# Attention output turned by VectorE and ScalarE instead of TensorE, from the fourth group on, in a fused DeltaNet and gated-MLP kernel

## The chip, the cores and the metric

The kernel runs on one core of a Trainium2 chip. The metric is the time of one execution on the device in microseconds (us); lower is better. In the profile PE is TensorE's matmul, PEld its weight load, DVE is VectorE, ACT is ScalarE, POOL is GpSimd and SP is SyncE.

## The reference, cut to what matters

```python
# q, k, v: (4, 8, 768, 48) = batch, heads, tokens, head size; all f32
k_n = k / (norm(k) + 1e-6)
for t in range(768):
    y[t]  = q[t] @ state                                   # per batch and head, state is 48 x 48
    state = state + beta[t] * outer(k_n[t], v[t] - k_n[t] @ state)
x   = y as (batch * token, 8 * 48)                         # 3072 x 384
out = (sigmoid(x @ w_gate) * (x @ w_val)) @ w_out          # 384 -> 1536 -> 384
```

## The kernel before

The 768 tokens are cut into 12 groups (0 to 11) of 64 tokens for each of the 4 batches, so a group has 256 tokens. Two kinds of work are woven into one instruction order that is written out by hand.

**The MLP of one group** is 12 tiles of the hidden width. For each, `gate_val` multiplies x of the group by 128 columns of both first weights (18 products of 128x256, into a two-buffered PSUM tile `gv`). ScalarE takes the sigmoid of one half (`sg`), VectorE multiplies it by the other half, ScalarE and VectorE split the product into two fp32r parts (`h`), and two tiles later `outp` multiplies them by the second weight (6 products of 128x384, into `po`). Every operand is split into a high and a low fp32r part, so x is a tile `xx` with a high half `xh` and a low half `xl`; the first product of a group reads `xh` and the second reads `xl`.

**The attention of the next group** runs in the gaps: key products (`gram`), norms and a triangular solve on VectorE (`solve`, many small operations on `X`, `gp` and `tmp`), the state's part (`rest`, `updates`, `advance`) and the output rows (`rows`). `rows` writes Y into PSUM (`yy`) with tokens on the partitions, and ScalarE copies it to `ys`, 128 x 768. The MLP needs Y with features on the partitions, in `xx`.

**The order.** A slot is one half of an MLP tile: an even slot issues `gate_val`, an odd slot issues `outp`. Lists say what else is issued in a slot: `plan[s]` right behind the matmuls, `late[s]` at its end. A group's MLP takes 24 slots; for group g, `w = 24 (g-1)` is the slot in which the MLP of the group before it starts, so its own starts at `w + 24`. For groups 3 to 11, `rows` and `advance` of the group stand in slot `w + 16`, and the turning of Y (`flip`) in `w + 18`. `scaling` puts 16 ScalarE operations on `kv` of a later group (`kv` times a norm, four per slot) into four slots. `spread` deals the small solve operations over slots by the room that the table `busy` leaves. No scheduler moves anything: every engine runs its queue in this order, and an instruction that waits holds up all behind it on its engine.

**Turning Y before the change.** `flip` runs twice, for 128 tokens each: three TensorE transpositions of 128x128 into PSUM (`pt`), then ScalarE rounds `pt` to `xh` and VectorE writes the rest to `xl`.

Of the kernel before, what the change touches and what calls it, by code (L numbers as in the profile page):

```python
# [12 lines left out]
F32 = mybir.dt.float32  # L13
F32R = mybir.dt.float32r
# [5 lines left out]
ALU = mybir.AluOpType  # L20
AX = mybir.AxisListType
PSUM = bass.MemoryType.PSUM

B, H, S, D = 4, 8, 768, 48
C = 64
GT = B * C
# [18 lines left out]

DM = H * D
FF = 1536
KC = DM // 128
# [7 lines left out]
def deltanet_gated_mlp(ctx: ExitStack, tc: tile.TileContext, kd, qd, kv, beta, words, out):  # L56
    nc = tc.nc
# [4 lines left out]
    wk = ctx.enter_context(tc.tile_pool(name="wk", bufs=1))  # L62
# [21 lines left out]
    state = [{} for _ in range(N)]  # L84
# [8 lines left out]
    def beat(ins):  # L93
        beats.append(ins)

    def busy_array(out, n, after=()):

        for i in range(n):
            ins = nc.tensor.matmul(out=out.rearrange("q a b -> q (a b)"), lhsT=flat[:, 0:128], rhs=flat, start=True, stop=True)  # L99
            if i < len(after):  # L100
                pace(ins, after[i])
# [20 lines left out]
    def load_group(g):  # L122
        load_k(g)
        load_q(g)
        load_rows(g, 1)
        load_rows(g, 0)
# [246 lines left out]
    def solve_halves(g):  # L373


        st = state[g]
        gp, gam = st["gp"], st["gam"]
        X = st["X"]
        H = wk.tile([128, 2, 8, 16], F32, name=f"H_{g}", tag="H", bufs=1)
        gs = wk.tile([128, 2, 16, 16], F32, name=f"gs_{g}", tag="gs", bufs=1)  # L380
        for b in range(2):
            nc.vector.tensor_tensor(out=H[:, b], in0=dmask[:, 8 * b:8 * b + 8, 16 * b:16 * b + 16],
                                    in1=gam[:, 16 * b:16 * b + 16].unsqueeze(1).to_broadcast([128, 8, 16]), op=ALU.mult)
            yield
            nc.vector.scalar_tensor_tensor(out=gs[:, b], in0=gp[:, 16 * b:16 * b + 16, 16 * b:16 * b + 16], scalar=-1.0,
                                           in1=gam[:, 16 * b:16 * b + 16].unsqueeze(1).to_broadcast([128, 16, 16]), op0=ALU.mult, op1=ALU.mult)
            yield
        for j in range(15, 0, -1):
            k, n = j // 2, 8 - j // 2
            tmp = wk.tile([128, 2, n, j], F32, name=f"tmp_{g}_{j}", tag="tmp", bufs=2)  # L390
            beat(nc.vector.tensor_tensor(out=tmp, in0=H[:, :, k:8, j:j + 1].to_broadcast([128, 2, n, j]),
                                         in1=gs[:, :, j:j + 1, 0:j].to_broadcast([128, 2, n, j]), op=ALU.mult))
            yield
            beat(nc.vector.tensor_tensor(out=H[:, :, k:8, 0:j], in0=H[:, :, k:8, 0:j], in1=tmp, op=ALU.add))
            yield
        for b in range(2):
            nc.vector.tensor_copy(out=X[:, 8 * b:8 * b + 8, 16 * b:16 * b + 16], in_=H[:, b])
            yield
        A, D, Z = (joints[g][:, i] for i in range(3))
        nc.vector.transpose(mt.rearrange("q c (k r) -> q k c r", r=2), X.rearrange("q k (c r) -> q k c r", r=2))  # L400
        yield
        pool, tag = (ps_aux, "aux") if g else (ps_gv, "gv")
        pz, pm = (pool.tile([128, CP, 32], F32, name=f"{n}_{g}", tag=tag) for n in ("pz", "pm"))

        def blocks(out, lhsT, rhs):
            for c in range(CP):
                for r in range(0, 128, 32):
                    nc.tensor.matmul(out=out[r:r + 32, c], lhsT=lhsT[r:r + 32, c], rhs=rhs[r:r + 32, c], start=True, stop=True)  # L408
        if g == 0:
            paced = beats[8::2]  # L410
            busy_array(pz, len(paced) + 4, after=paced)
        if g:
            blocks(pz, A, mt)
        else:
            for c in range(CP):
                for r in range(0, 128, 64):
                    nc.tensor.matmul(out=pz[r:r + 64, c], lhsT=wide[r:r + 64, c], rhs=mt[r:r + 64, c], start=True, stop=True)
        if g == 0:
            busy_array(pm, 2)
        yield  # L420
        nc.vector.transpose(D.rearrange("q c t -> q (c t)"), mt.rearrange("q c t -> q (c t)"))
        nc.scalar.copy(Z, pz)
        yield
        blocks(pm, D, Z)
        if g == 0:
            gap.append(ps_gv.tile([128, J, C], F32, name="gap", tag="gv"))
            busy_array(gap[0], 3)
        yield
        st["joint"] = nc.vector.tensor_tensor(out=mt, in0=mt, in1=pm, op=ALU.subtract)
        yield  # L430
# [101 lines left out]
    def flip(g, c):  # L532

        st = state[g]
        if c == 0:
            xx = wk.tile([128, 2, KC, GT], F32R if g else F32, name=f"xx_{g}", tag=f"xx{(g + 1) % 2}", bufs=1)
            st["xh"], st["xl"] = (xx[:, i] for i in range(2))
        xh, xl, ys = st["xh"], st["xl"], st["ys"][:, c].rearrange("p h e d -> p (h e d)")
        pt = ps_aux.tile([128, KC, 128], F32, name=f"pt_{g}_{c}", tag="aux")
        for k in range(KC):  # L540
            nc.tensor.transpose(pt[:, k], ys[:, k * 128:(k + 1) * 128], ident)  # L541
        ts = slice(c * 128, (c + 1) * 128)
        if g == 0:
            (nc.vector.tensor_copy if c else nc.scalar.copy)(out=xh[:, :, ts], in_=pt)  # L544
            return
        nc.scalar.copy(xh[:, :, ts], pt)
        nc.vector.tensor_tensor(out=xl[:, :, ts], in0=pt, in1=xh[:, :, ts].bitcast(F32), op=ALU.subtract)


    def gate_val(g, f):  # L550
        st = state[g]
        x = (st["xh"], st["xl"])
        st["gv", f] = pg = ps_gv.tile([128, 2, GT], F32, name=f"gv_{g}_{f}", tag="gv")
        for o, w in ((0, "g"), (1, "v")):
            for k in range(KC):
                if g == 0:
                    nc.tensor.matmul(out=pg[:, o], lhsT=parts[w, f][:, k * 128:(k + 1) * 128], rhs=x[0][:, k], start=k == 0, stop=k == KC - 1)  # L557
                    continue
                for q, (a, b) in enumerate(((0, 0), (0, 1), (1, 0))):
                    nc.tensor.matmul(out=pg[:, o], lhsT=parts[w, f][:, a, k * 128:(k + 1) * 128], rhs=x[b][:, k], start=(k == 0 and q == 0), stop=(k == KC - 1 and q == 2))  # L560
# [43 lines left out]
    plan = collections.defaultdict(list)  # L604
    late = collections.defaultdict(list)

    def steps(gen, n=1):
        def fn():
            for _ in range(n):
                next(gen, None)  # L610
        return fn
# [10 lines left out]
    def chain(*gens):  # L622
        for q in gens:
            yield from q
# [5 lines left out]
    def scaling(g, s):  # L630
        for i in range(4):
            plan[s + i].append(steps(scalings[g], 4))
# [88 lines left out]
    busy = collections.Counter()  # L721

    def mask_later(g, s):
        def fn():
            masks = masked(g)
            take(masks, 2)
            plan[s + 1].insert(0, steps(masks, 2))
        late[s].append(fn)
        for i in range(2):
            busy[s + i] += 1.4  # L730
# [9 lines left out]
    for g in range(N):  # L740
        w = W * (g - 1)
        if g == 0:
            late[3].append(lambda: advance(0))
            continue
        up, at_rows = (13, 19) if g < 3 else (10, 16)
        at_rest = {1: 8, 2: 28}.get(g, w + 6)
        late[at_rest].append(lambda g=g: rest(g))
        for step in range(3):
            late[w + up + 2 * step].append(lambda g=g, step=step: updates(g, step))
        late[w + at_rows].append(lambda g=g: rows(g))  # L750
        late[w + at_rows].append(lambda g=g: advance(g))
        for c in range(2):
            late[w + at_rows + 2].append(lambda g=g, c=c: flip(g, c))
            busy[w + at_rows + 2] += 0.6
        busy[at_rest] += 1.1
        busy[w + up + 2] += 1.1
        busy[w + at_rows] += 1.1
        busy[w + at_rows + 1] += 1.1
        if g == 1:
            mask_later(1, 11)  # L760
        else:
            if g > 2:
                plan[w - 27].append(lambda g=g: load_group(g))
            gram_later(g, {2: 3, 3: 32}.get(g, w - 18))
            mask_later(g, w + 1 if g == 2 else w - 12)
            if g > 2:
                solves.append((g, w - 13 if g == 3 else w - 14, w + 9))
            scaling(g, {2: 25, 3: 43}.get(g, w - 7))
    spread(chain(norms(2), halves2), NORMS + 36, 8, 25, lambda s: max(0.1, 1.6 - busy[s]))
    for at in (26, 29, 30, 30, 31):  # L770
        plan[at].append(steps(halves2))
# [74 lines left out]
```

## Time and profile before

| what | value |
|---|---|
| median of 3 runs | 649.55 us (645.4 to 651.54) |
| the profiled execution: time, span of its instructions | 646.87 us, 645.2 us |
| mean granted TensorE clock | 0.994 |
| busy share of the span: PE, PEld, DVE, ACT, POOL | 96%, 90%, 72%, 50%, 2% |
| chain that ended last: PE, DVE, ACT | 91%, 4%, 2% |
| TensorE transpositions of Y (`pt`) | 72, in 12 groups |

The chain is the work that ended last, followed back from the last instruction to what released each step. A share in it says where the end is set; a busy share only says how full an engine is.

### The profile page before, as it was taken

To read this page: it belongs to the slowest core of one execution; us is meant where nothing else is said; L and a number is where in the kernel's file an instruction comes from. 1 tells how busy PE (TensorE), PEld (TensorE's weight loads), DVE (VectorE), ACT (ScalarE), POOL (GpSimd) and SP (SyncE) were. 2 spreads that over 40 slices of the span, in tenths; PEclk is the share of its full clock that TensorE was granted. 3 is DMA by queue.
4 is the path that set the end of the run, shared out by engine and by line. 5 is a ranking of instruction groups with operands and counts; after the bars stand their busy time and mean duration, and the time that the engine had idled before them with its cause. 6 is when DMAs were issued, how large, how long until landed. Compare 5 with 4: busy or idle time off the path is not lost.

```text
span 645.2 us, 24064 instructions
## 1 busy us (share of the span) xinstructions
PE 622.1 (96%) x10548; PEld 582.1 (90%) x10556; DVE 467.3 (72%) x1443; ACT 320.6 (50%) x870; POOL 11.3 (2%) x30
## 2 busy tenths in 40 slices
PE   6789799999999999999999999999999999999996
PEld 4457578889999999999999999999999999999996
DVE  5878687688987977977977977977977977952221
ACT  4879584577345346246256256256255355334222
POOL 6000000000000000000000000000000000000000
PEclk9889999999999999999999999999999999999999
DMA  9595722202103102103102112112113100100101
GB/s 267 188 295 181 230 76 84 53 2 85 38 16 84 37 16 86 28 25 84 26 27 85 25 28 85 26 28 85 25 28 85 25 4 3 25 3 3 25 1 25
DMA packets 17769, 41.07 MB, mean 64 GB/s; under 512 B 4224, under 2 KB 7296, under 8 KB 17664
## 3 DMA queue, kind: packets, MB, share of 16 engines
q1 hardware_dynamic: 17664, 39.53, 21.3%
q8 instruction: 83, 1.36, 0.9%
q14 instruction: 22, 0.18, 0.1%
HBM read 34.80 MB, written 4.72 MB: 61 GB/s over the span
## 4 chain that ended last, share of the span: by engine, by line
PE 91%; DVE 4%; ACT 2%; issue 2%; DMA 1%; ACTq 0%; SPq 0%; DVEq 0%
PE gv L560 44%; PE po L591 23%; PE gv L557 3%; PE pu L476 3%; PE yy L502 2%; PE yy L505 2%; PE po L585 2%; PE pg L291 2%; PE pp L319 2%; PE pk L445 2%; PE pd L523 2%; PE pk L468 1%; PE pt L541 1%; PE pm L408 1%; PE pz L99 1%
## 5 line engine op out<-in xcount | busy, mean ns | idle before, releaser
L560 PE MATMUL gv<-xx,w 128*128 128x256 f32 x2376 | 307.5, 283 | 0.0
L560 PEld LDWEIGHTS gv<-xx,w 128*128 128x128 f32 x2376 | 301.3, 191 | 0.9
L591 PE MATMUL po<-w,h 128*128 128x384 f32 x792 | 166.2, 345 | 0.0
L565 ACT ACTIVATE sg<-gv 128x256 f32<-128x256 f32 x144 | 55.3, 384 | 203.6 <-PE gv L560 187.2
L591 PEld LDWEIGHTS po<-w,h 128*128 128x128 f32 x792 | 133.3, 188 | 3.1
L566 DVE TENSOR_TENSOR sg<-sg,gv 128x256 f32<-128x256 f32 x144 | 60.3, 419 | 78.0 <-ACT sg L565 77.5
L571 ACT CAST h<-sg 128x256 fp32r<-128x256 f32 x132 | 53.5, 405 | 51.5 <-DVE sg L566 50.2
L350 DVE TENSOR_TENSOR X<-X,tmp 128x126 f32<-128x126 f32 (+22 forms) x279 | 71.3, 256 | 9.0
L347 DVE TENSOR_TENSOR tmp<-X,gp 128x126 f32<-128x126 f32 (+22 forms) x279 | 71.0, 254 | 7.9
L576 DVE TENSOR_TENSOR h<-sg,h 128x256 fp32r<-128x256 f32 x132 | 55.0, 417 | 28.6 <-ACT h L571 28.6
L482 ACT COPY su<-pu 32x384 f32<-32x384 f32 x92 | 43.3, 471 | 15.1 <-PE pu L476 13.9
L279 ACT ACTIVATE kv<-kv,mq 128x48 f32<-128x48 f32 x192 | 48.2, 329 | 0.0
L324 DVE TENSOR_TENSOR kqp<-pp,pmask 64x512 f32<-64x512 f32 x48 | 32.2, 686 | 7.3 <-PE pp L319 6.3
L530 DVE TENSOR_TENSOR su<-su,pd 48x384 f32<-48x384 f32 x40 | 22.1, 552 | 19.3 <-PE pd L523 18.8
L303 ACT COPY G<-pg 32x256 f32<-32x256 f32 (+1 forms) x69 | 25.4, 368 | 18.1 <-PE pg L291 16.8
L557 PE MATMUL gv<-xx,u 128*128 128x256 f32 x144 | 33.7, 385 | 0.3 <-ACT xx L544 0.3
L557 PEld LDWEIGHTS gv<-xx,u 128*128 128x128 f32 x144 | 26.6, 190 | 4.9 <-ACT xx L544 0.8
L456 DVE TENSOR_TENSOR R<-kv,pk 128x384 f32<-128x384 f32 x44 | 22.4, 550 | 1.4 <-PE pk L445 1.4
L476 PEld LDWEIGHTS pu<-R,mt 32*32 32x32 f32 x1408 | 16.5, 105 | 4.9 <-issue 1.7
L212 ACT CAST w<-u 128x384 fp32r<-128x384 f32 x36 | 18.0, 508 | 5.7 <-DVE w L219 5.6
L476 PE MATMUL pu<-R,mt 32*32 32x48 f32 x1408 | 19.4, 202 | 0.9 <-DVE kqp L324 0.9
L189 ACT ACTIVATE raw<-raw 128x384 int32<-128x384 uint16 x36 | 19.9, 553 | 0.2 <-DMA raw<-in_words_dram 0.2
(104 smaller groups left out, 515.7 us busy)
## 6 DMA issues: line engine op xcount, KB each, us to landing
raw<-in_words_dram SPq DMA_DIRECT2D x36, 384.0 KB, 5.6
kv<-in_kv_dram SPq DMA_DIRECT2D x24, 384.0 KB, 4.3
kqp<-in_qd_dram SPq DMA_DIRECT2D x24, 256.0 KB, 4.2
kqp<-in_kd_dram SPq DMA_DIRECT2D x24, 192.0 KB, 3.5
out_dram<-ot SPq DMA_DIRECT2D x48, 96.0 KB, 2.2
beta<-in_beta_dram SPq DMA_DIRECT2D x12, 16.0 KB, 4.0
```

The lines of the kernel that those rows point to most:

```text
L279: nc.scalar.activation(V[:, c], V[:, c], AF.Copy, scale=mq[:, c, 0:1])
L347: nc.vector.tensor_tensor(out=tmp, in0=X[:, k:16, j:j + 1].to_broadcast([128, n, j]), in1=gp[:, j:j + 1, 0:j].to_broadcast([128, n, j]), o ...
L350: nc.vector.tensor_tensor(out=X[:, k:16, 0:j], in0=X[:, k:16, 0:j], in1=tmp, op=ALU.add)
L476: nc.tensor.matmul(out=pu[0 if g else x][r:r + 32, j], lhsT=mt[r:r + 32, e * J + j], rhs=R[e][r:r + 32, j], start=True, stop=True)
L482: nc.scalar.copy(su[r:r + 32, 3 if x else e], pu[0][r:r + 32])
L557: nc.tensor.matmul(out=pg[:, o], lhsT=parts[w, f][:, k * 128:(k + 1) * 128], rhs=x[0][:, k], start=k == 0, stop=k == KC - 1)
L560: nc.tensor.matmul(out=pg[:, o], lhsT=parts[w, f][:, a, k * 128:(k + 1) * 128], rhs=x[b][:, k], start=(k == 0 and q == 0), stop=(k == KC - ...
L565: nc.scalar.activation(h, st["gv", f][:, 0], AF.Sigmoid)
L566: nc.vector.tensor_tensor(out=h, in0=h, in1=st["gv", f][:, 1], op=ALU.mult)
L571: nc.scalar.copy(hh[:, 0], st["sg", f])
L576: nc.vector.tensor_tensor(out=hh[:, 1], in0=st["sg", f], in1=hh[:, 0].bitcast(F32), op=ALU.subtract)
L591: nc.tensor.matmul(out=po[s], lhsT=hh[:, a, ts], rhs=parts["o", f][:, w], start=(f == 0 and q == 0), stop=(f == NF - 1 and q == 2))
```

## The change

For groups 3 to 11 `flip` is replaced by a new generator, `turn`. VectorE transposes all of `ys` in blocks of 32x32, in one instruction (`yt`). Blocks that stay on their 32 partitions this way still have to change places, so ScalarE copies them between partitions: 16 copies of 32 partitions x 192 elements, each from 32 partitions of `yt` to 32 partitions of a tile `x`. Then one ScalarE instruction rounds all of `x` (128 x 768) to `xh`, and one VectorE instruction writes `xl`. The copies are dealt four per slot over slots `w + 17` to `w + 20`, `xh` and `xl` stand in `w + 21`. The scaling of `kv` moves three slots back, from `w - 7` to `w - 4` (for the next group these are slots 20 to 23 of the same count). `x` takes the buffer of `ys`; `yt` shares a buffer with two solve tiles of groups 0 to 2. Groups 0 to 2 keep `flip`.

```diff
--- before.py
+++ after.py
@@ -376,8 +376,9 @@
         st = state[g]
         gp, gam = st["gp"], st["gam"]
         X = st["X"]
-        H = wk.tile([128, 2, 8, 16], F32, name=f"H_{g}", tag="H", bufs=1)
-        gs = wk.tile([128, 2, 16, 16], F32, name=f"gs_{g}", tag="gs", bufs=1)
+        hg = wk.tile([128, 768], F32, name=f"hg_{g}", tag="hg", bufs=1)
+        H = hg[:, 0:256].rearrange("q (b k t) -> q b k t", b=2, k=8)
+        gs = hg[:, 256:768].rearrange("q (b i t) -> q b i t", b=2, i=16)
         for b in range(2):
             nc.vector.tensor_tensor(out=H[:, b], in0=dmask[:, 8 * b:8 * b + 8, 16 * b:16 * b + 16],
                                     in1=gam[:, 16 * b:16 * b + 16].unsqueeze(1).to_broadcast([128, 8, 16]), op=ALU.mult)
@@ -546,6 +547,25 @@
         nc.scalar.copy(xh[:, :, ts], pt)
         nc.vector.tensor_tensor(out=xl[:, :, ts], in0=pt, in1=xh[:, :, ts].bitcast(F32), op=ALU.subtract)
 
+
+    def turn(g):
+
+        st = state[g]
+        xx = wk.tile([128, 2, KC, GT], F32R, name=f"xx_{g}", tag=f"xx{(g + 1) % 2}", bufs=1)
+        st["xh"], st["xl"] = (xx[:, i] for i in range(2))
+        yt = wk.tile([128, 2, DM // 32, 32], F32, name=f"yt_{g}", tag="hg", bufs=1)
+        nc.vector.transpose(yt.rearrange("q c m s -> q (c m s)"), st["ys"].rearrange("q c h e d -> q (c h e d)"))
+        yield
+        x = wk.tile([128, KC, 2, 4, 32], F32, name=f"x_{g}", tag="ys", bufs=1)
+        for q in range(4):
+            for a in range(4):
+                nc.scalar.copy(x[32 * q:32 * q + 32, :, :, a].rearrange("q k c s -> q c k s"), yt[32 * a:32 * a + 32, :, q::4])
+                yield
+        x = x.rearrange("q k c a s -> q k (c a s)")
+        nc.scalar.copy(st["xh"], x)
+        yield
+        nc.vector.tensor_tensor(out=st["xl"], in0=x, in1=st["xh"].bitcast(F32), op=ALU.subtract)
+        yield
 
     def gate_val(g, f):
         st = state[g]
@@ -749,9 +769,17 @@
             late[w + up + 2 * step].append(lambda g=g, step=step: updates(g, step))
         late[w + at_rows].append(lambda g=g: rows(g))
         late[w + at_rows].append(lambda g=g: advance(g))
-        for c in range(2):
-            late[w + at_rows + 2].append(lambda g=g, c=c: flip(g, c))
-            busy[w + at_rows + 2] += 0.6
+        if g < 3:
+            for c in range(2):
+                late[w + at_rows + 2].append(lambda g=g, c=c: flip(g, c))
+                busy[w + at_rows + 2] += 0.6
+        else:
+            turned = turn(g)
+            plan[w + 17].append(steps(turned, 1))
+            for at, n in ((17, 4), (18, 4), (19, 4), (20, 4), (21, 2)):
+                late[w + at].append(steps(turned, n))
+            busy[w + 17] += 0.6
+            busy[w + 21] += 0.6
         busy[at_rest] += 1.1
         busy[w + up + 2] += 1.1
         busy[w + at_rows] += 1.1
@@ -765,7 +793,7 @@
             mask_later(g, w + 1 if g == 2 else w - 12)
             if g > 2:
                 solves.append((g, w - 13 if g == 3 else w - 14, w + 9))
-            scaling(g, {2: 25, 3: 43}.get(g, w - 7))
+            scaling(g, {2: 25, 3: 43}.get(g, w - 4))
     spread(chain(norms(2), halves2), NORMS + 36, 8, 25, lambda s: max(0.1, 1.6 - busy[s]))
     for at in (26, 29, 30, 30, 31):
         plan[at].append(steps(halves2))
```

The next pieces are of group 5, where the change moves instructions. In the names the first number is the group: `h_4_8` is tile 8 of the MLP of group 4.

ScalarE, from the copies of Y on, before the change:

```order
L511 COPY ys_5_5206<-yy_5_0_5156 128x8x48
L511 COPY ys_5_5206<-yy_5_1_5157 128x8x48
L279 ACTIVATE kv_6_4500<-kv_6_4500,mq_6_5125 128x48 x4
L571 CAST h_4_8_5259<-sg_4_8_5153 128x256
L279 ACTIVATE kv_6_4500<-kv_6_4500,mq_6_5125 128x48 x4
L565 ACTIVATE sg_4_9_5286<-gv_4_9_5261 128x256
L546 CAST xx_5_5289<-pt_5_0_5290 128x3x128
L546 CAST xx_5_5289<-pt_5_1_5296 128x3x128
L279 ACTIVATE kv_6_4500<-kv_6_4500,mq_6_5125 128x48 x4
```

ScalarE, the same place after the change, from the last MLP operation ahead of the first copies (`x` from `yt`) to `xh`:

```order
L591 CAST h_4_8_5271<-sg_4_8_5167 128x256
L562 COPY x_5_5273<-yt_5_5268 32x2x3x32 x4
L585 ACTIVATE sg_4_9_5304<-gv_4_9_5278 128x256
L562 COPY x_5_5273<-yt_5_5268 32x2x3x32 x4
L591 CAST h_4_9_5325<-sg_4_9_5304 128x256
L562 COPY x_5_5273<-yt_5_5268 32x2x3x32 x4
L279 ACTIVATE kv_6_4508<-kv_6_4508,mq_6_5140 128x48 x4
L585 ACTIVATE sg_4_10_5361<-gv_4_10_5331 128x256
L562 COPY x_5_5273<-yt_5_5268 32x2x3x32 x4
L279 ACTIVATE kv_6_4508<-kv_6_4508,mq_6_5140 128x48 x4
L591 CAST h_4_10_5391<-sg_4_10_5361 128x256
L565 CAST xx_5_5267<-x_5_5273 128x768
```

`xh` stood two instructions behind the second group of `kv` scalings; it now stands behind 16 copies, two groups of scalings and four MLP operations.

VectorE, from the state's update (`su`) on, before the change:

```order
L530 TENSOR_TENSOR su_79<-su_79,pd_5_1_5210 48x384
L530 TENSOR_TENSOR su_79<-su_79,pd_5_0_5209 48x384 x2
L530 TENSOR_TENSOR su_79<-su_79,pd_5_1_5210 48x384
L347 TENSOR_TENSOR tmp_6_31_5257<-X_6_5127,gp_6_4883 128x31
L350 TENSOR_TENSOR X_6_5127<-X_6_5127,tmp_6_31_5257 128x31
L576 TENSOR_TENSOR h_4_8_5259<-sg_4_8_5153,h_4_8_5259 128x256
L566 TENSOR_TENSOR sg_4_9_5286<-sg_4_9_5286,gv_4_9_5261 128x256
L547 TENSOR_TENSOR xx_5_5289<-pt_5_0_5290,xx_5_5289 128x3x128
L547 TENSOR_TENSOR xx_5_5289<-pt_5_1_5296,xx_5_5289 128x3x128
```

VectorE after the change, the same place:

```order
L531 TENSOR_TENSOR su_79<-su_79,pd_5_1_5224 48x384
L531 TENSOR_TENSOR su_79<-su_79,pd_5_0_5223 48x384 x2
L531 TENSOR_TENSOR su_79<-su_79,pd_5_1_5224 48x384
L557 STREAM_TRANSPOSE yt_5_5268<-ys_5_5220 128x768
L336 SCALAR_TENSOR_TENSOR gp_6_4898<-gp_6_4898,gam_6_5137 128x16x16
L347 TENSOR_TENSOR tmp_6_31_5297<-X_6_5142,gp_6_4898 128x31
```

The transposition stands right behind the four updates of the state. `xl` now comes behind the product of tile 10 (`sg_4_10`) and three solve operations:

```order
L586 TENSOR_TENSOR sg_4_10_5361<-sg_4_10_5361,gv_4_10_5331 128x256
L350 TENSOR_TENSOR X_6_5142<-X_6_5142,tmp_6_25_5358 128x4x25
L347 TENSOR_TENSOR tmp_6_24_5388<-X_6_5142,gp_6_4898 128x96
L350 TENSOR_TENSOR X_6_5142<-X_6_5142,tmp_6_24_5388 128x4x24
L567 TENSOR_TENSOR xx_5_5267<-x_5_5273,xx_5_5267 128x768
```

On TensorE the six transpositions (`pt_5_0` and `pt_5_1`, between `gv_4_9` and the next `po`) are gone for groups 3 to 11; all else there keeps its order, and the SyncE queue of transfers keeps its own.

## The prediction

> **What bounds the kernel now.** First the page: busy shares, the chain that ended last, the group of `gate_val` products; then one stretch of the steady state (busy us of PE, PEld, DVE, ACT and POOL in 53 us, then the granted clock).
>
> ```profile
> PE   622.1 (96%) x10548; PEld 582.1 (90%) x10556; DVE 467.3 (72%) x1443; ACT 320.6 (50%) x870; POOL 11.3 (2%) x30
> PE 91%; DVE 4%; ACT 2%; issue 2%; DMA 1%; ACTq 0%; SPq 0%; DVEq 0%
> L560 PE MATMUL gv<-xx,w 128*128 128x256 f32 x2376 | 307.5, 283 | 0.0
> 259.00:312.00 53.00, 53.00 (x869) 51.84 (x868) 42.42 (x137) 23.86 (x67) 0.00 (x0) 1.00 0.16 42
> ```
>
> TensorE sets the end: it is 91% of the chain, and its products of 128x256 wait 0.0 us. So TensorE work taken out is time gained, as long as nothing reaches TensorE late for it. By the average there is room for the new work: in 53 us VectorE is free for 10.6 and ScalarE for 29.1. But the engines run their queues in order, so I follow one group, group 5, through TensorE's timeline (start, length, what).
>
> ```profile
> 296.33 0.94 PE L523 MATMUL pd<-su,kv 64*48 64x48 f32 x64
> 297.19 1.32 PE L591 MATMUL po<-w,h 128*128 128x384 f32 x6
> 298.36 2.33 PE L560 MATMUL gv<-xx,w 128*128 128x256 f32 x18
> 300.52 0.82 PE L541 MATMUL pt<-ident,ys 128*128 128x128 f32 x6
> 301.09 1.29 PE L591 MATMUL po<-w,h 128*128 128x384 f32 x6
> 302.23 2.31 PE L560 MATMUL gv<-xx,w 128*128 128x256 f32 x18
> 304.38 1.22 PE L591 MATMUL po<-w,h 128*128 128x384 f32 x6
> 305.44 2.33 PE L560 MATMUL gv<-xx,w 128*128 128x256 f32 x18
> 308.66 2.33 PE L560 MATMUL gv<-xx,w 128*128 128x256 f32 x18
> ```
>
> The `gv` at 308.66 is the first product of group 5, the reader of its `xx`. All ahead of it is MLP work of group 4.
>
> **Removed from TensorE.** From one `gv` to the next are 3.21 us (302.23 to 305.44), and 3.87 us (298.36 to 302.23) where the six transpositions lie between: they cost 0.65 us a group, not their 0.82 us of busy time. For nine groups that is 5.9 us. If nothing else moved, the profiled 646.87 us would become 641.0.
>
> **The new way to `xx`.** Before, the rest of `xx` was written by 302.6 (next fence), 6 us ahead of its reader. Now it hangs on this chain. VectorE's two rows and its prices:
>
> ```profile
> 297.36 2.25 DVE L530 TENSOR_TENSOR su<-su,pd 48x384 f32<-48x384 f32 x4 [2.17 <-PE pd L523]
> 301.57 1.02 DVE L547 TENSOR_TENSOR xx<-pt,xx 128x384 fp32r<-128x384 f32 x2
> L240 DVE STREAM_TRANSPOSE gp<-G 128x1024 f32<-128x1024 f32 x12 | 14.8, 1235 | 0.1
> L352 DVE STREAM_TRANSPOSE mt<-X 128x512 f32<-128x512 f32 x9 | 6.4, 714 | 0.3
> L576 DVE TENSOR_TENSOR h<-sg,h 128x256 fp32r<-128x256 f32 x132 | 55.0, 417 | 28.6 <-ACT h L571 28.6
> L456 DVE TENSOR_TENSOR R<-kv,pk 128x384 f32<-128x384 f32 x44 | 22.4, 550 | 1.4 <-PE pk L445 1.4
> ```
>
> The transposition is queued behind the four state updates, which wait for TensorE's `pd` and end at 299.61. Between 714 ns for 512 columns and 1235 for 1024, 768 columns take 0.97: it ends at 300.58. The final `xl`, 768 columns of a two-input operation, is extended from 417 ns (256) and 550 (384): 0.95.
>
> ScalarE then has, in its queue up to `xh`: 16 copies, 8 scalings of `kv`, two sigmoids, two `h` and `xh`. Its prices by form, and rows of its timeline:
>
> ```profile
> L565 ACT ACTIVATE sg<-gv 128x256 f32<-128x256 f32 x144 | 55.3, 384 | 203.6 <-PE gv L560 187.2 <-PE gv L557 14.2 <-PE pt L541 2.0
> L571 ACT CAST h<-sg 128x256 fp32r<-128x256 f32 x132 | 53.5, 405 | 51.5 <-DVE sg L566 50.2
> L212 ACT CAST w<-u 128x384 fp32r<-128x384 f32 x36 | 18.0, 508 | 5.7 <-DVE w L219 5.6
> L308 ACT COPY L<-pg 32x256 f32<-32x256 f32 x48 | 17.4, 362 | 0.6
> L360 ACT ACTIVATE wide<-G,under 32x256 f32<-32x256 f32 x4 | 2.9, 734 | 2.7 <-DVE under L159 2.6
> 277.61 1.49 ACT L308 COPY L<-pg 32x256 f32<-32x256 f32 x4
> 296.82 1.01 ACT L279 ACTIVATE kv<-kv,mq 128x48 f32<-128x48 f32 x4
> 297.74 0.39 ACT L571 CAST h<-sg 128x256 fp32r<-128x256 f32 x1
> 298.03 1.01 ACT L279 ACTIVATE kv<-kv,mq 128x48 f32<-128x48 f32 x4
> ```
>
> From 405 ns (256) and 508 (384), both out of SBUF, a column costs 0.80 ns, so a copy of 192 columns takes 0.35 us and `xh` with 768 takes 0.82. No row shows a copy between partitions. The nearest are the four copies of 32 partitions at 277.61: 1.49 us, each after the end of the one before, where instructions on all 128 partitions overlap by 0.1 (`h` at 297.74 takes 0.39, its successor starts after 0.29). The new copies change their 32 partitions every time as well, so I take them as not overlapping: 0.36 each, 16 x 0.36 = 5.76. With the overlap it would be 0.26 each (16 x 0.10 = 1.6 us less). The dearest row is `wide`, 734 ns for 256 columns, with a scattered write that the new copies lack; by its slope a copy takes 0.60, 3.8 us more. I stay with the row of the same kind.
>
> Sum: 5.76 + `kv` 2 x 0.92 (296.82 to 297.74) + sigmoids 0.77 + `h` 0.81 + `xh` 0.82 = 10.0 us. The sigmoids and `h` have their inputs by then, since TensorE runs ahead. So `xh` is ready at 310.6 and `xl` at 311.5; VectorE has only three solve steps behind tile 10's product and waits there.
>
> TensorE would ask for `xl` with its second product, at 308.66 - 0.65 + 0.12 = 308.13. It waits **3.4 us in each of groups 3 to 10**. What is late next is VectorE's queue: its solve steps run without a gap behind `xl`, which ends 4.7 us after the place where it stood before (306.8), while TensorE is 2.75 us later.
>
> ```profile
> 306.56 0.26 DVE L350 TENSOR_TENSOR X<-X,tmp 128x96 f32<-128x96 f32 x1
> 311.88 2.33 PE L560 MATMUL gv<-xx,w 128*128 128x256 f32 x18
> 315.62 0.41 DVE L566 TENSOR_TENSOR sg<-sg,gv 128x256 f32<-128x256 f32 x1
> ```
>
> The product for the `gv` that ended at 314.2 started 1.4 us behind it; 1.9 us more makes 3.3. TensorE needs that buffer again 4.3 us behind the end (`po`, `gv`, `po`: 1.06, 2.15, 1.06 between the starts at 302.23, 304.38 and 305.44), so a start within 3.9 us is hidden, and I add nothing; every us beyond would be lost once a group. VectorE's idle 2.17 us before the state updates then absorbs its net new work (0.97 + 0.95 - 1.02 = 0.9).
>
> Group 11 has no state update and no `kv` behind it:
>
> ```profile
> 587.25 0.95 ACT L511 COPY ys<-yy 128x384 f32<-128x384 f32 x2 [1.25 <-PE yy L505]
> 599.04 2.32 PE L560 MATMUL gv<-xx,w 128*128 128x256 f32 x18
> ```
>
> Its transposition ends at 589.2. Behind it stand 10.0 - 1.84 us of ScalarE work, but tile 10's sigmoid holds it until 594.6; then four copies, `h`, `xh` and `xl` end near 598.9, against 599.04 - 0.65 + 0.12 = 598.5. It gains about 0.25.
>
> **The clock.** TensorE's idle time has a price of its own. The start of the trace has gaps; cut into stretches of 3.41 us they read:
>
> ```profile
> 2.64:6.06 3.42, 1.77 (x50) 1.59 (x54) 0.75 (x1) 0.00 (x0) 3.34 (x4) 1.00 1.01 250
> 16.30:19.72 3.42, 1.56 (x4) 0.48 (x5) 2.97 (x14) 3.23 (x8) 0.00 (x0) 1.00 1.05 400
> 19.72:23.14 3.42, 3.32 (x8) 0.90 (x9) 2.90 (x15) 3.37 (x14) 0.00 (x0) 0.50 0.57 219
> 33.38:36.80 3.42, 1.56 (x53) 0.80 (x51) 2.51 (x10) 1.76 (x5) 0.00 (x0) 1.00 0.93 281
> 36.80:40.22 3.42, 3.08 (x46) 1.62 (x49) 2.73 (x7) 2.72 (x6) 0.00 (x0) 0.50 1.05 261
> ```
>
> Two stretches with 1.56 us of TensorE work (1.86 idle) are each followed by a whole stretch at clock 0.50; one with 1.77 is not. The edges lie on one grid (16.30 and 33.38 are five stretches apart). A wait of 3.4 us covers at least 1.7 us of one stretch of this grid, nearly always over 1.75, so I expect a stretch at half clock after nearly every wait. It costs 1.7 us if it starts after the wait and down to 0.9 if it starts within it; I take 1.45. [...]
>
> **The sum.** 646.87 + 8 x (3.4 - 0.65 + 1.45) - 0.25 = 680.2, say **680 us**. The median shown, 649.55, lies 2.7 above the profiled time; I add nothing for it.
>
> **The rivals.**
> 1. *The wait comes, the clock stays at 1.00.* For it: the two low stretches had small products and fillers, not a dense stream around one hole. Against: the rows above. 646.87 + 8 x 2.75 - 0.25 = 668.6. Chance 0.17.
> 2. *The copies overlap*, 0.26 each: the wait shrinks to 1.8, under the 1.86 idle that halved the clock. 646.87 + 8 x 1.15 - 0.65 = 655.4. Against it stand the four copies at 277.61. [...] Chance 0.13.
> 3. *Faster: ScalarE's chain fits in front of the reader.* The place is `xh` at the end of slot `w + 21`, the price 9 x 0.65 = 5.9 us, so 641.0. It decides where the 10.0 us shrink by 3.4, to 0.15 us for a copy. For it: both engines have free time on average. Against: even 48 columns on `kv` take 0.23 each (0.92 / 4), with overlap. Chance 0.08.
> 4. *The copies cost 0.60*, as `wide`: the wait is 7.2 us, with the clock 1.7 more; 646.87 + 8 x 8.25 = 713. Chance 0.05.
> 5. *Wait and saving cancel* (a copy of 0.19, wait 0.65): 647. Chance 0.05.
>
> **How the numbers follow.** The forecast has 0.52. Its own range is 672 to 690: a wait of 3.0 to 4.0, with 1.3 to 1.7 for the clock in seven or eight groups. The range from 653 to 692 takes in rivals 1 and most of 2, and leaves out 3, 4 and 5. About 1% is what a measurement of this kernel can tell from no change. Rival 3 and a little of 5 give faster 0.09; the rest of 5 and half of rival 2 (655.4 is 0.9% above the median shown) give same 0.11; the rest is slower, 0.80.
>
> **What the changed profile would show.** No `pt` in groups 3 to 11, 18 left. The 16 copies in runs of four taking 1.4 us. TensorE's waits naming `xx`, written by VectorE, eight times some 3.4 us. `gv` of each group's first tile at a clock of 0.50 for up to 3.4 us in most groups. The forecast is wrong if a run of four copies takes near 1.0 us or over 2 us, if TensorE does not wait at `xx`, or if the clock row stays at 1.00 behind the waits.

## The result and the profile after

The changed kernel takes **685.42 us** (median of 6 runs, 683.18 to 688.28), the kernel before 647.3 (6 runs): a ratio of 1.0587, with a 95% interval of 1.0552 to 1.0622, some 38 us slower. The profiled execution took 683.18 us with a span of 681.5, 36.3 us more than the span before.

The page of the changed kernel, in the lines that answer to those of before (busy shares, chain by engine, the `gate_val` products), and its new copies:

```profile
PE 635.7 (93%) x10502; PEld 589.4 (86%) x10502; DVE 474.3 (70%) x1443; ACT 368.6 (54%) x1005; POOL 11.3 (2%) x30
PE 73%; ACT 14%; DVE 8%; issue 2%; DMA 1%; ACTq 0%; SPq 0%; DVEq 0%
L580 PE MATMUL gv<-xx,w 128*128 128x256 f32 x2376 | 318.0, 288 | 23.9 <-ACT xx L565 18.9
L562 ACT COPY x<-yt 32x192 f32<-32x192 f32 x144 | 50.4, 350 | 30.9 <-DVE yt L557 29.0
```

ScalarE was 2% of the chain and is 14%: it now sets the end in places, though it is busy for only 54% of the span. The `gv` products, which never waited, wait 23.9 us. TensorE's waits name the two halves of `xx`, in groups 3 to 10 (8 times for `xh`), and in group 11 for `xl` alone (us in total, times, longest):

```profile
PE gv L580 <- ACT xx L565: 18.9, 8, 2.4
PE gv L580 <- DVE xx L567: 5.0, 9, 0.6
```

Group 5 in TensorE's, ScalarE's and VectorE's timelines, from the transposition to the reader of `xx`:

```profile
313.76 1.22 PE L611 MATMUL po<-w,h 128*128 128x384 f32 x6
314.82 2.33 PE L580 MATMUL gv<-xx,w 128*128 128x256 f32 x18
316.98 1.22 PE L611 MATMUL po<-w,h 128*128 128x384 f32 x6
320.60 0.38 PE L580 MATMUL gv<-xx,w 128*128 128x256 f32 x1 [2.40 <-ACT xx L565]
321.59 2.29 PE L580 MATMUL gv<-xx,w 128*128 128x256 f32 x17 [0.61 <-DVE xx L567]
...
310.68 1.44 ACT L562 COPY x<-yt 32x192 f32<-32x192 f32 x4 [4.17 <-DVE yt L557]
312.02 0.37 ACT L585 ACTIVATE sg<-gv 128x256 f32<-128x256 f32 x1
312.41 1.44 ACT L562 COPY x<-yt 32x192 f32<-32x192 f32 x4
313.87 0.41 ACT L591 CAST h<-sg 128x256 fp32r<-128x256 f32 x1
314.30 1.43 ACT L562 COPY x<-yt 32x192 f32<-32x192 f32 x4
315.75 1.01 ACT L279 ACTIVATE kv<-kv,mq 128x48 f32<-128x48 f32 x4
316.67 0.36 ACT L585 ACTIVATE sg<-gv 128x256 f32<-128x256 f32 x1
317.05 1.43 ACT L562 COPY x<-yt 32x192 f32<-32x192 f32 x4
318.51 1.01 ACT L279 ACTIVATE kv<-kv,mq 128x48 f32<-128x48 f32 x4
319.42 0.39 ACT L591 CAST h<-sg 128x256 fp32r<-128x256 f32 x1
319.72 0.83 ACT L565 CAST xx<-x 128x768 fp32r<-128x768 f32 x1
...
307.38 2.25 DVE L531 TENSOR_TENSOR su<-su,pd 48x384 f32<-48x384 f32 x4 [2.92 <-PE pd L524]
309.66 0.98 DVE L557 STREAM_TRANSPOSE yt<-ys 128x768 f32<-128x768 f32 x1
320.58 0.96 DVE L567 TENSOR_TENSOR xx<-x,xx 128x768 fp32r<-128x768 f32 x1 [2.33 <-ACT xx L565]
```

ScalarE waits 4.17 us for the transposition and then runs without a gap until `xh` is written, at 320.55. TensorE finished `po` and would have gone on at 316.98 + 1.06 = 318.04. Its second product, due 0.12 us later, starts at 321.59: **3.43 us late** (3.16 in group 3, whose wait for `xh` is 2.14 and not 2.40 us).

The clock, in the 3.41 us stretches of the grid on which it changes in this trace (TensorE's busy us, instructions, granted clock), for the waits of groups 4, 5, 6, 7 and 8:

```profile
265.39:268.80 3.41, 1.51 (x10) 1.00 0.00 0
268.80:272.21 3.41, 3.41 (x16) 0.50 0.00 0
316.59:320.00 3.41, 1.61 (x11) 1.00 0.01 2
320.00:323.41 3.41, 2.20 (x16) 1.00 0.00 0
371.20:374.61 3.41, 1.73 (x12) 1.00 0.00 0
374.61:378.03 3.42, 3.42 (x15) 0.50 0.00 0
422.40:425.81 3.41, 1.04 (x6) 1.00 0.00 0
425.81:429.23 3.42, 2.86 (x13) 0.50 0.00 0
429.23:432.64 3.41, 3.41 (x15) 0.50 0.02 5
477.02:480.43 3.41, 0.91 (x4) 1.00 0.00 0
480.43:483.85 3.42, 2.92 (x13) 0.50 0.00 0
483.85:487.26 3.41, 3.41 (x28) 1.00 0.00 0
```

Six of the eight waits (groups 4 and 6 to 10) are followed by half clock, two of them (groups 7 and 10) for two stretches: eight stretches in all. What they cost stands in TensorE's timeline, from the second product of a group to the first one of its third tile. These are 6.41 us in groups 3 and 5 (321.59 to 328.00), where no half clock follows. In groups 4, 6 and 9, with one stretch wholly behind the wait, they are 7.92, 7.91 and 7.90 us: 1.5 us more for 3.41 us at clock 0.50. In group 8, whose only stretch begins while TensorE still waits, they are 7.69 us, and in groups 7 and 10, with a first one of this kind and a second one, 9.06 us. The clock's share is 3 x 1.5 + 1.28 + 2 x 2.65 = 11.1 us.

The start of the program has its share too. The MLP of group 1, ahead of all that the change moves on TensorE, starts 2.1 us later (the kernel before, then the changed one):

```profile
106.45 2.60 PE L560 MATMUL gv<-xx,w 128*128 128x256 f32 x18
108.55 2.61 PE L580 MATMUL gv<-xx,w 128*128 128x256 f32 x18
```

In the nine traces of this case this start lies anywhere from 103.9 to 110.5 us, and with one trace of each kernel no part of the 2.1 us can be put down to the change. So the 36.3 us are: 7 x (3.43 - 0.65) + (3.16 - 0.65) = 22.0 in groups 3 to 10, less 0.26 in group 11, plus 11.1 of clock and 2.1 of start, together 34.9. Of the 1.4 us that are left, 0.8 lie at `pd` of group 5: the next `po` starts 1.64 us after it (305.60 to 307.24) and not 0.86 (296.33 to 297.19 in the kernel before), with 0.49 us of idle time that the profile puts down to "issue". The other 0.6 stay open.

### The profile page after: what moved, and what is told of

Read it like the earlier page. It is cut to its first block, busy times and chain, and to the rows that moved or that the text cites. A ratio compares the mean times of both kernels' runs of the same rounds, so it can differ in the third digit from the quotient of the medians.

```text
span 681.5 us, 24056 instructions
## 1 busy us (share of the span) xinstructions
PE 635.7 (93%) x10502; PEld 589.4 (86%) x10502; DVE 474.3 (70%) x1443; ACT 368.6 (54%) x1005; POOL 11.3 (2%) x30
## 4 chain that ended last, share of the span: by engine, by line
PE 73%; ACT 14%; DVE 8%; issue 2%; DMA 1%; ACTq 0%; SPq 0%; DVEq 0%
PE gv L580 35%; PE po L611 16%; ACT x L562 7%; PE gv L577 4%; PE pu L477 3%; ACT kv L279 3%; DVE su L531 3%; PE pp L319 2%; PE yy L503 2%; PE po L605 2%; PE yy L506 2%; PE pg L291 2%; PE pk L446 2%; PE pd L524 2%; PE pk L469 1%
## 5 line engine op out<-in xcount | busy, mean ns | idle before, releaser
L580 PE MATMUL gv<-xx,w 128*128 128x256 f32 x2376 | 318.0, 288 | 23.9 <-ACT xx L565 18.9
L580 PEld LDWEIGHTS gv<-xx,w 128*128 128x128 f32 x2376 | 308.7, 195 | 29.3 <-ACT xx L565 21.5
L611 PE MATMUL po<-w,h 128*128 128x384 f32 x792 | 170.0, 351 | 0.0
L611 PEld LDWEIGHTS po<-w,h 128*128 128x128 f32 x792 | 137.4, 194 | 3.4 <-issue 0.3
L562 ACT COPY x<-yt 32x192 f32<-32x192 f32 x144 | 50.4, 350 | 30.9 <-DVE yt L557 29.0
L577 PE MATMUL gv<-xx,u 128*128 128x256 f32 x144 | 36.1, 405 | 0.3 <-DVE xx L545 0.3
L577 PEld LDWEIGHTS gv<-xx,u 128*128 128x128 f32 x144 | 28.3, 202 | 5.6 <-ACT xx L545 0.8
L567 DVE TENSOR_TENSOR xx<-x,xx 128x768 fp32r<-128x768 f32 x9 | 8.6, 958 | 20.9 <-ACT xx L565 20.9
```

The source lines that it names most:

```text
L562: nc.scalar.copy(x[32 * q:32 * q + 32, :, :, a].rearrange("q k c s -> q c k s"), yt[32 * a:32 * a + 32, :, q::4])
L611: nc.tensor.matmul(out=po[s], lhsT=hh[:, a, ts], rhs=parts["o", f][:, w], start=(f == 0 and q == 0), stop=(f == NF - 1 and q == 2))
```

## The experiments

Theory A, the prediction's: ScalarE's queue between the transposition and `xh` is longer than the TensorE work that covers it, and the half clock follows from TensorE's idle time. Theory B: the wait is VectorE's, by the transposition's place behind the state updates. Theory C: the clock falls for another reason.

**The transposition first.**

```diff
         late[w + at_rows].append(lambda g=g: rows(g))
+        if g >= 3:
+            turned = turn(g)
+            late[w + at_rows].append(steps(turned, 1))
         late[w + at_rows].append(lambda g=g: advance(g))
 ...
-            turned = turn(g)
-            plan[w + 17].append(steps(turned, 1))
```

> VectorE's transposition of Y stands ahead of the four state updates instead of behind them; all else as in the changed kernel. It can then start when ys is written, about 3.4 us earlier against TensorE. Theory A (ScalarE's queue is too long: TensorE waits for what is left of it): the first four copies move into ScalarE's idle time, but the sigmoid of tile 9 behind them still waits for TensorE's product of that tile, so only the first four copies leave the chain. From that product's end to xl are 0.4 + 3 x 1.44 + 0.4 + 0.9 + 0.4 + 0.9 + 0.3 + 0.8 + 1.0 = 9.4 us against 7.5 us of TensorE work: a wait of about 1.9 us in groups 3 to 10, too short for the half clock in most groups. Time 646.9 + 8 x (1.9 - 0.65) - 0.25 = about 657 us. Theory B (the wait is VectorE's, whose transposition is queued behind the state updates): the wait is gone, 641 us. Theory C (the clock falls for another reason than the waits): 670 us or more.

Measured: 666.15 us, ratio to the kernel before 1.0269 (1.0222 to 1.0316). In group 5, ScalarE's and TensorE's timelines:

```profile
305.22 1.43 ACT L562 COPY x<-yt 32x192 f32<-32x192 f32 x4 [0.74 <-DVE yt L557]
308.95 0.38 ACT L585 ACTIVATE sg<-gv 128x256 f32<-128x256 f32 x1 [2.29 <-PE gv L580]
...
315.19 1.22 PE L611 MATMUL po<-w,h 128*128 128x384 f32 x6
317.54 0.38 PE L580 MATMUL gv<-xx,w 128*128 128x256 f32 x1 [1.14 <-ACT xx L565]
318.53 2.30 PE L580 MATMUL gv<-xx,w 128*128 128x256 f32 x17 [0.61 <-DVE xx L567]
```

The transposition comes early now, but ScalarE does only four copies and then stands 2.29 us at the sigmoid of tile 9. The reader is 318.53 - (315.19 + 1.06 + 0.12) = 2.2 us late, so theory B falls as the whole cause: VectorE's place was part of it, the rest is ScalarE's. The time is 9 us above what theory A expected: the wait is 2.2 and not 1.9 (2 us over eight groups), and it still halved the clock behind three of the eight waits, which I had thought too short for it (4.5 us, at the 1.5 us of a stretch in the changed kernel). The remaining 2.5 us lie at the start of the program: in this execution the MLP of group 1 starts at 109.21, 2.8 us later than in the kernel before, with 17 us of half clock before 82 us against 6.8.

**The scaling of `kv` later.**

```diff
-            scaling(g, {2: 25, 3: 43}.get(g, w - 4))
+            scaling(g, {2: 25, 3: 43}.get(g, w))
```

> The scaling of kv moves from slots w-4..w-1 to w..w+3, behind xh; all else as in the changed kernel. Theory A: the two runs of four scalings leave the chain, 1.84 us less, so the wait falls from 3.4 to 1.6 us and is too short for the half clock: 646.9 + 8 x (1.6 - 0.65) - 0.25 = about 654 us. Theory B (VectorE's place in the order sets the wait): nothing changes, 685 us. Theory C (the clock falls for another reason): about 668 us, with the half-clock stretches still there.

Measured: 658.31 us, 1.0142 (1.0083 to 1.0201), 4 us above the expectation of theory A and 27 below that of B. The waits for `xx`:

```profile
PE gv L580 <- DVE xx L567: 5.1, 9, 0.6
PE gv L580 <- ACT xx L565: 4.7, 8, 0.6
```

The wait for `xh` went from 18.9 us to 4.7: 1.8 us a group, as the two runs of `kv` take. No half clock follows any wait. What lies above the expectation is mostly the start again: the MLP of group 1 starts at 110.49 in this execution, 4.0 us later than in the kernel before.

**Both.** The two edits above together.

> Both: transposition ahead of the state updates, and kv scaled behind xh. Theory A: from the end of tile 9's product to xl are 9.4 - 1.84 = 7.6 us against 7.5 us of TensorE work, so the wait is nearly gone (0 to 0.2 us) and the 0.65 us of six transpositions a group is gained: 641 to 643 us. Theory B: 641 us as well. Theory C: 655 us, the clock still falling.

Measured: 645.46 us, 0.9948 (0.9927 to 0.9969), above the 641 to 643 expected; the kernel before took 648.46 in these runs, 1.6 us more than the expectation starts from. The wait for `xl` that is left is small:

```profile
306.41 2.29 PE L580 MATMUL gv<-xx,w 128*128 128x256 f32 x17 [0.25 <-DVE xx L567]
```

It makes the product 0.4 us late in each group; 9 x (0.65 - 0.4) = 2.3 us of gain lie within what the ratio shows (3.4 us, interval 2.0 to 4.7). That wait is twice the 0.2 us that was expected at most.

**Fillers in the wait.**

```diff
         elif t < N:
+            if f == 0 and 3 <= t < N - 1:
+                busy_array(ps_aux.tile([128, J, C], F32, name=f"fill_{t}", tag="aux"), 14)
             gate_val(t, f)
```

> The changed kernel with 14 products of 128x512 bf16 on constant data, written to a spare PSUM tile that nobody reads, ahead of the first product of groups 3 to 10: 14 x 0.21 = 3.0 us of work inside the wait of 3.4 us. Theory A: the wait stays as it is and the clock stays at 1.00 behind it: 646.9 + 8 x (3.4 - 0.65) - 0.25 = about 669 us, some 14 us less than the changed kernel. Theory C (the half clock does not come from idle time): 685 us. If the fillers lengthen the wait instead: over 690 us.

Measured: 669.78 us, 1.0318 (1.0262 to 1.0374). TensorE at the start of group 5 (one record of the 14 is missing):

```profile
314.57 1.22 PE L611 MATMUL po<-w,h 128*128 128x384 f32 x6
315.63 3.19 PE L99 MATMUL fill<-dmask 128*128 128x512 bf16 x13
318.47 0.47 PE L580 MATMUL gv<-xx,w 128*128 128x256 f32 x1
319.18 2.30 PE L580 MATMUL gv<-xx,w 128*128 128x256 f32 x17 [0.24 <-DVE xx L567]
```

The second product is as late as in the changed kernel (319.18 against 314.57 + 1.06 + 0.12 = 315.75, 3.4 us), but no half clock follows in any group. Of the loss 15.6 us are gone by the medians and 12.2 by the two profiled executions (683.18 and 671.01 us), where 11.1 were read above as the clock's share. Theory C falls. Work that nobody reads made the changed kernel faster.

**The scaling alone, in the kernel before.**

```diff
-            scaling(g, {2: 25, 3: 43}.get(g, w - 7))
+            scaling(g, {2: 25, 3: 43}.get(g, w - 4))
```

> The kernel before with one part of the change alone: the scaling of kv three slots later (w-4), Y still turned by TensorE. Theory A (the later scaling costs only because it stands ahead of xh in ScalarE's queue): without the 16 copies ScalarE has idle time there and xx is ready before, so no change, 645 to 650 us, as the kernel before. Rival (the moved scaling collides with the MLP's sigmoids by itself): slower by 5 us or more.

Measured: 647.04 us, 0.9982 (0.9961 to 1.0003): nothing that can be told from no change. The later scaling costs only because it stands ahead of `xh`.

**The copies without the move between partitions.**

```diff
-                nc.scalar.copy(x[32 * q:32 * q + 32, :, :, a].rearrange("q k c s -> q c k s"), yt[32 * a:32 * a + 32, :, q::4])
+                cols = slice(192 * a, 192 * a + 192)
+                nc.scalar.copy(x.rearrange("q k c a s -> q (k c a s)")[:, cols], yt.rearrange("q c m s -> q (c m s)")[:, cols])
```

> The changed kernel with the 16 copies on all 128 partitions, 192 columns each, from yt to x without the change of partitions: the blocks are not put into their places, so this leaves out that part of the computation; number, columns and place of the copies stay. If the copies did not overlap because each one moves to other partitions: 0.26 instead of 0.36 us each, runs of four in about 1.15 us, the wait falls from 3.4 to about 1.8 to 2.1 us, some of the half-clock stretches vanish: 655 to 665 us. If copies out of SBUF never overlap: runs of four in 1.44 us, 685 us.

Measured: 653.03 us, 1.0083 (1.0052 to 1.0114), 2 us below the expectation. The reader in group 5 is 1.4 us late, where 1.8 to 2.1 were expected, and no half clock follows any wait. ScalarE's timeline and the lengths of a copy (ns, min, median, max):

```profile
304.54 1.11 ACT L563 COPY x<-yt 128x192 f32<-128x192 f32 x4 [4.45 <-DVE yt L557]
L563 ACT COPY x<-yt x144: 337/352/357, 204.2 to 603.8; 128x192 f32<-128x192 f32 x144
```

One copy is as long as in the changed kernel (352 ns against 350), but four take 1.11 us and not 1.44. So neither the number, the columns nor the memory of the copies keeps them from overlapping. This run changed three things together: the partitions on which a copy starts, their count (128 for 32) and the order of the blocks. The timeline of the changed kernel, above, helps to part them. Behind the four copies to partitions 0 to 31, `sg` starts 0.1 us before the last of them ends (312.02 against 310.68 + 1.44 = 312.12); behind the four to partitions 32 to 63, `h` does not start before the end (313.87 against 312.41 + 1.44 = 313.85). Both follow copies of 32 partitions with the same order of blocks, so these two alone do not prevent the overlap, and the start partition fits. Whether the side that is read or the side that is written counts, no run separates: `sg` reads PSUM, `h` reads SBUF as the copies do.

**Copies where ScalarE is idle.** On top of the two edits of "both":

```diff
-            for at, n in ((17, 4), (18, 4), (19, 4), (20, 4), (21, 2)):
+            for at, n in ((17, 8), (18, 4), (19, 4), (20, 2)):
 ...
-            busy[w + 21] += 0.6
+            busy[w + 20] += 0.6
```

> As e3_both, with the copies dealt 8, 4 and 4 over slots w+17 to w+19 and xh and xl in w+20. Theory A: eight copies fit into ScalarE's idle time behind the transposition, xl is ready 1 to 2 us ahead of its reader, TensorE never waits for it, and what is left is the removal of six transpositions a group: 9 x 0.65 = 5.9 us less than the kernel before, ratio 0.991, about 642.5 us where the kernel before takes 648.5. Rival (the removed transpositions were hidden beside other TensorE work): no better than e3_both, 645.5.

Measured: **642.35 us**, 0.9922 (0.9896 to 0.9948), 5.1 us less than the kernel before by the ratio (interval 3.4 to 6.7), where 5.9 were expected. ScalarE, VectorE and the reader on TensorE in group 5:

```profile
299.29 2.88 ACT L562 COPY x<-yt 32x192 f32<-32x192 f32 x8 [0.74 <-DVE yt L557]
308.11 0.96 DVE L567 TENSOR_TENSOR xx<-x,xx 128x768 fp32r<-128x768 f32 x1 [0.44 <-ACT xx L565]
310.38 1.85 PE L580 MATMUL gv<-xx,w 128*128 128x256 f32 x14
```

Eight copies now lie in the time in which ScalarE waited for tile 9's product, `xl` is written at 309.07, and its reader at 310.38 does not wait. It beats the kernel before and the changed kernel: the idea of the change is sound, and its place in the queues was not.

## Why the prediction held

The forecast was 680 us, the measured median is 685.42, within the range.

- *What TensorE saves.* 72 transpositions became 18. 0.65 us for six, and not their 0.82 us of busy time, is borne out by the version with early copies: 9 x 0.65 = 5.9 lies in its 3.4 to 6.7, and 9 x 0.82 = 7.4 does not.
- *The price of a copy.* The trace of before had none between partitions; of the three rows that bounded it, the four copies of 32 partitions were the right ones: 0.36 us each by 1.44 for four, as taken. Rival 2, the overlap, is what the copies without the move show, at 653 us (655.4 was its price). Four copies took 1.44 us with the move between partitions and 1.11 without it.
- *The wait.* 3.4 us were worked out and 3.43 measured in group 5, with the transposition at 0.98 (0.97 taken), `xh` at 0.83 (0.82) and `xl` at 0.96 (0.95). Group 11 lost 0.39 of its 0.65 us, as said. TensorE's waits name ScalarE's `xh` for the first 2.4 us and VectorE's `xl` only for the last 0.6, where the prediction had named `xl` for all of it. No wait of TensorE from group 3 on names another tile: VectorE's later queue stayed hidden.
- *The clock.* This term came near: 1.45 us a wait were taken and 11.1 / 8 = 1.39 came, 0.5 us less over eight groups. A stretch wholly behind its wait cost 1.5 us, where 1.7 was taken. That the term came so near is in part luck. The step "a stretch at half clock after nearly every wait" failed in both directions: behind two waits, which the grid split, no half clock followed (in group 5 a stretch with 1.61 us of work, 1.80 idle, kept the clock, where the prediction let 1.75 idle be enough), and two were followed by two stretches. The fillers put that term alone at 12 to 16 us. Rival 1, 668.6, in which the clock stays at 1.00, is out: the clock fell behind six of eight waits, and the stretches ahead of a fall had 0.91 to 1.73 us of work.
- *The rest.* The profiled execution, 683.18 us, is 3.0 above the sum: 2.1 of the start, which the sum took as unchanged, and the 1.4 that are left in the sum of the 36.3, less 0.5 of clock. The median lies another 2.2 above it: the profiled execution was the fastest of the six and had the highest mean granted clock (0.970, the others 0.960 to 0.968). The sum made no claim on that.

## What to carry to other kernels

An engine that is free for half of the time can still be late (ScalarE, busy for 54% of the span, kept TensorE waiting 2.4 us a group): add up what its queue holds between the moment the input is there and the moment the output is read, and compare that with the work that covers it. When a saving is moved to another engine, give it the place in that engine's queue where it now stands idle, and move what is not urgent (here `kv`) behind what is read next. A wait of the matrix engine can cost more than its length: here waits of 3.4 us brought half clock in six cases of eight, those of 2.2 us in three of eight, those of 1.6 us in none. Constant work in the hole tells how much more (here 12 to 16 us of the loss).

## What the runs showed of the hardware

In this case's traces the clock changes at the edges of a grid of 3.41 us, and half clock comes behind stretches with little TensorE work, but the busy time in the records gives no sharp limit. In the dense part of the changed kernel, stretches with 0.91 to 1.54 us of work and one with 1.73 brought it, those with 1.61 (group 5) and 1.98 (group 3) did not. At its start one with 1.84 did (16.21 to 19.62 us), and in the kernel before one with 1.63 did not (70.91 to 74.33).

Half clock can last for a second stretch, and what decides it stays open. In groups 7 and 10 TensorE was busy for 2.86 and 2.85 us of the first stretch at 0.50 and a second one followed; in group 8 it was busy for 2.92 and none followed. Less work in the first one is not the whole reason: at the start of the program one with 3.28 was followed by a second as well.

```profile
74.24:77.66 3.42, 3.28 (x61) 0.50 0.31 116
77.66:81.07 3.41, 3.41 (x10) 0.50 0.00 0
```
